# Thresholded attention and a gated MLP on one core: the MLP's products three steps earlier, in another order

## The chip, the cores and the metric

The kernel runs on one core of a Trainium2 chip. The metric is the time of one execution on the device, in microseconds (us). The profile is that of one such execution, and the trace is its list of instructions with their starts and durations. The engines are named as in the profile: PE is the matrix engine, PEld its weight loads, DVE the vector engine, ACT the scalar engine, POOL the general-purpose engine, and SP the queue that issues nearly all DMAs.

## The reference

Eight batches of eight heads, 576 rows of 64 numbers per head, all in float32. The first half is an attention whose weights are cut off below the row's maximum less `tau` (0.02):

```python
scores = scale * np.matmul(q, k.transpose(0, 1, 3, 2))
thresh = np.max(scores, axis=-1, keepdims=True) - tau
scores = np.where(scores >= thresh, scores, -1000000000.0)
scores = scores - np.max(scores, axis=-1, keepdims=True)
attn = np.exp(scores)
attn = attn / (np.sum(attn, axis=-1, keepdims=True) + 1e-09)
attn_out = np.matmul(attn, v)
```

The heads of a batch are put side by side (576 rows of 512 numbers, `x`), and the second half is a gated MLP on it:

```python
h = np.maximum(x @ w_in, 0.0)                      # 512 -> 1024
u, v = h[..., :512], h[..., 512:]
v_n = (v - mean(v)) / np.sqrt(var(v) + 1e-06)      # over the last axis
v_s = np.einsum('ts,bsd->btd', w_spatial, v_n) + b_spatial[None, :, None]
out = (u * v_s) @ w_out
```

## The kernel before

**Attention in 144 steps.** Two heads of one batch make a pair `i`, 32 pairs in all. A step `(i, c)` takes 128 of the 576 score rows of a pair. The last 64 rows of two neighbouring pairs share one step, `c = 4`, so an even pair has four steps and an odd pair has five, in the order 4, 0, 1, 2, 3. In `step()` the engines get this, in this order:

- PE: `scores()` (L545 and L550) into one of two score tiles `s` of three PSUM banks each; then the matmuls of the step's jobs.
- DVE: the row maxima `negm` (L586), for `c` = 2 and 4 a small correction (L590), and later the cut `p` (L567), which belongs to the step before and only exists for `c` = 0, 1, 3.
- ACT: the evacuations of the step's jobs, then `e` from the scores (L609; L603 with an `exp` of the whole row, L605, where `c` is 2 or 4). The pass over `s` is what frees the score tile for the step after next.
- SP: the transposes `pT<-p` by DMA, loads and outputs.

**Jobs.** Each step has a list `fs` of jobs, each with matmuls into one PSUM bank (`mm`) and an evacuation (`ev`) on ACT ("act") or DVE ("dve"). The list is sorted with the act jobs first. The matmuls of the first two jobs stand right behind the scores on PE, and their act evacuations stand on ACT ahead of the step's `e`. The matmuls of a third job stand behind the first two on PE. A third job's act evacuation is put into `held` and runs at the start of the next step. In the 144 steps a job's bank comes from `ps_f`, which has two banks in rotation: a job's matmuls wait until the job before the last has been evacuated.

Jobs that belong to the attention: `qk_main` and `qk_rem` transpose q and k of the next pair (L245, L260; evacuated by ACT at L250, L252, L263), `pv` and `pv_rest` multiply the weights by v (L289, L294; evacuated by DVE at L301, L303). `x_pe` (L367, ACT L374) transposes some pairs of `x`, and `ws_pe` (L388, ACT L392) the five pieces of `w_spatial`.

Jobs of the MLP of a batch:

- `v`, five per batch: `moe_v` (L418, ACT L428), with normalisation afterwards on ACT (L442, two steps later) and POOL; the fifth also carries the last output rows of the batch before (`ends`, L403 and L406, with a further copy at L432).
- `s`, five: `moe_s` (L490, or L495 for the fifth, which has 20 short matmuls), multiplied by `u` on DVE (L504, L507).
- `u`, five: `moe_u` (L460, or L465 for the fifth), ACT L475 or L477.
- `o`, four: `moe_o` (L519), ACT L524, then a DMA to the output.

**The order.** One batch is four pairs, so 18 steps. Job number `j` of `ORDER` of batch `b` goes to step `LAG + 18 * b + j`; `v` and `u` are those of batch `b`, `s` and `o` those of batch `b - 1`. What would fall behind step 143 goes into `last` and runs after the steps. Loads and casts of the weights are `chores` at fixed steps.

**The tail.** After step 143 the six banks of the score tiles join `ps_f` as eight banks for the jobs (`bank()`). `run()` takes the rest of the jobs of batch 6, the last `pv` and `x_pe` jobs, and `s` of batch 6; then `last_gmlp` does `v`, its normalisation, `s` and the output of batch 7, with `u` of batch 7 and the four `o` of batch 6 in between.

Of the kernel before, what the change touches and what calls it, by code (L numbers as in the profile page):

```python
# [17 lines left out]
def kernel(  # L18
# [21 lines left out]
    NPAIR = B * H // 2  # L40
# [187 lines left out]
    def bank16():  # L228

        return bank(BF16, 640)  # L230
# [77 lines left out]
    def pv(i, part):  # L308

        b, hp = divmod(i, HP)  # L310
        hold = {}

        def mm():
            t = hold["t"] = bank()
            for k in range(2):
                weigh(t, 130 * k, pts[i, part][:, k], v_ring[i % 4])

        def ev():
            if part == 0:
                xns[i] = xp.tile([P, 4, P], BF16, name="xn")  # L320
            xn = xns[i]
            divide(hold["t"], [(slice(0, P), 0, 4,
                                xn[:, 2 * part:2 * part + 2, :].rearrange(
                                    "p c (h d) -> p (c h) d", h=2))])
            if part == 1:
                if hp == 0:
                    xts[b] = xtp.tile([P, 4, 640], BF16, name="xT")
                if i in x_on_pe:
                    return
                sends.append(lambda: nc.sync.dma_start_transpose(  # L330
                    out=xts[b][:, hp, 0:512].rearrange("p (c s) -> p c s", s=P),
                    in_=xn.rearrange("p c d -> p (c d)")))
        return "dve", mm, ev
# [25 lines left out]
    def x_pe(i, rest=False):  # L359

        b, hp = divmod(i, HP)
        hold = {}

        def mm():
            t = hold["t"] = bank16()
            for c in range(4):
                nc.tensor.transpose(out=t[:, c * P:(c + 1) * P], in_=xns[i][:, c, :],  # L367
                                    identity=identb)
            if rest:
                nc.tensor.transpose(out=t[:, 512:640], in_=xns["rest", i // 2], identity=identb)  # L370

        def ev():
            if not rest:
                nc.scalar.copy(out=xts[b][:, hp, 0:512], in_=hold["t"][:, 0:512])  # L374
                return
            nc.scalar.copy(out=xts[b][:, hp, 0:256], in_=hold["t"][:, 0:256])
            nc.vector.tensor_copy(out=xts[b][:, hp, 256:512], in_=hold["t"][:, 256:512])
            nc.vector.tensor_copy(out=xts[b][:, hp - 1, 512:640], in_=hold["t"][:, 512:640])
        return "act", mm, ev
# [102 lines left out]
    def moe_s(b, f):  # L482
        hold = {}
        vn = vn_ring[b % 2]

        def mm():
            t = hold["t"] = bank()
            if f < 4:
                for c in range(5):
                    nc.tensor.matmul(out=t, lhsT=vn[:, c, f * P:(f + 1) * P],  # L490
                                     rhs=wsT[:, c, 0:512], start=(c == 0), stop=(c == 4))
            else:
                for g in range(4):
                    for c in range(5):
                        nc.tensor.matmul(out=t[:, g * 64:g * 64 + 64],  # L495
                                         lhsT=vn[:, c, g * P:(g + 1) * P],
                                         rhs=wsT[:, c, 512:576], start=(c == 0), stop=(c == 4))

        def ev():
            if f == 0:  # L500
                gs[b] = mw.tile([P, 4, S], BF16, name="gT")
            t = hold["t"]
            if f < 4:
                nc.vector.tensor_tensor(out=gs[b][:, f, 0:512], in0=t, in1=us[b][:, f, 0:512],  # L504
                                        op=ALU.mult)
            else:
                nc.vector.tensor_tensor(out=gs[b][:, :, 512:576],  # L507
                                        in0=t[:, 0:256].rearrange("p (f s) -> p f s", f=4),
                                        in1=us[b][:, :, 512:576], op=ALU.mult)
        return "dve", mm, ev  # L510
# [228 lines left out]
    chores[13] = (load_w_in, 3)  # L739
    for gs_, f in (((4, 5, 6, 17), shape_w_in),  # L740
                   ((20, 25, 30), load_ws), ((24, 26, 29, 31, 34), shape_ws),
                   ((36, 41, 46, 51), load_w_o), ((39, 44, 49, 54), shape_w_o)):
        chores.update({g: (f, j) for j, g in enumerate(gs_)})

    LAG = 26
    ORDER = "vsvsvsvssuvuouououo"
    jobs, last = {}, []
    for b in range(B):  # L750
        n = dict.fromkeys("vuso", 0)
        for j, t in enumerate(ORDER):
            f = {"v": moe_v, "u": moe_u, "s": moe_s, "o": moe_o}[t]
            if t in "uv" or b:
                g = LAG + PER * b + j
                job = (f, b - (t in "so"), n[t])
# [5 lines left out]
    Z = B - 1  # L762
# [1 line left out]
    for g, j in x_jobs:  # L764
        jobs.setdefault(g, []).append((x_pe, j))
    for j in range(5):
        jobs.setdefault((29, 33, 34, 42, 44)[j], []).append((ws_pe, j))
    with tc.manual_schedule():
        for w in (0, 1):
            for f in load(0, 1, w, (nc.sync, nc.scalar)[w]):  # L770
                f()
        make_identity(nc, identf)
        clear()
        nc.vector.memset(ntau, -float(tau))
        nc.vector.memset(mhalf, -0.5)
        nc.scalar.activation(out=ctau, in_=ntau, func=ACT.Exp)
        nc.vector.tensor_copy(out=identb, in_=identf)
        for w in (0, 1):
            for f in load(1, 1, w):
                f()  # L780
        for f in load(0, 2, 2):
            f()
        for j in range(3):
            load_w_in(j)
        for _ in range(14):
            nc.tensor.transpose(out=ps_f.tile([P, 512], F32, name="f")[:, 0:P], in_=identf,
                                identity=identf)
        shape_first()
        first()
        shape_qk(1)  # L790
        queue = []
        for g, (i, c) in enumerate(steps):
            if c == 2 and i + 2 < NPAIR:
                shape_qk(i + 2)
            if c == 0:
                shape_v(i)
            if c == 0 and i % 2 and i + 3 < NPAIR or g == 0:
                for w in range(3):
                    queue.extend(load(i + (3 if g else 2), 2, w))
            if g in chores:  # L800
                chores[g][0](chores[g][1])
            fs, small_ones = [], []
            if i + 1 < NPAIR and c < 3:
                fs.append(qk_rem(i + 1) if c == 1 else qk_main(i + 1, c // 2))
            if i and c == (2 if i % 2 else 3):
                fs.append(pv(i - 1, 0))
            if i > 1 and c == 4:
                fs.append(pv(i - 2, 1))
            if i % 2 and c == 3:
                fs.append(pv(i - 1, 1))  # L810
            if i % 2 and i > 1 and c == 1:
                small_ones = [pv_rest(i // 2 - 1)]
                fs += small_ones
            fs += [f(*a) for f, *a in jobs.get(g, [])]
            fs.sort(key=lambda f: (f[0] == "dve", f in small_ones))
            sends += queue[:1 if g > 3 else 2]
            del queue[:1 if g > 3 else 2]
            step(i, c, fs)

        def run(*fs):  # L820
            for f in fs:
                f[1]()
                f[2]()
                for f in sends:
                    f()
                sends.clear()
        while held:
            held.pop(0)()
        mask()
        inner.close()  # L830
        wide.append(ctx.enter_context(tc.tile_pool(name="ps_t", bufs=6, space=PSUM,
                                                  reuse_waits="tile")))
        for _, f in later:
            f()
        last = [f(b, j) for f, b, j in last]
        run(last[0], pv_rest(NPAIR // 2 - 1), *last[1:3], x_pe(NPAIR - 2), *last[3:6],
            pv(NPAIR - 1, 0), *last[6:], pv(NPAIR - 1, 1), moe_s(Z - 1, 0), moe_s(Z - 1, 1),
            x_pe(NPAIR - 1, True), *[moe_s(Z - 1, j) for j in range(2, 5)])
        rest = last_gmlp(Z)
        next(rest)  # L840
        run(moe_u(Z, 0), moe_u(Z, 1))
        next(rest)
        run(*[moe_u(Z, j) for j in range(2, 5)], *[moe_o(Z - 1, j) for j in range(4)])
        next(rest)
        next(rest, None)
# [35 lines left out]
```

## Time and profile before

| | us |
|---|---|
| median of three runs | 480.41 |
| the three runs | 479.06, 480.41, 481.51 |
| profiled execution, its own time | 480.41 |
| span of its instructions | 478.6 |

The profiled execution's own time is that of the median, and 1.8 us of it lie around the span. The granted clock of PE was 0.995 of full speed over the span. Steps can be found in the trace by the 144 instructions of L586: the first starts at 9.2 us, the last at 437.7 us. "Step of the cycle" below is the number of a step modulo 18.

### The profile page before, as it was taken

Reading aid. Unit: us, or ns where it says so; the run is one execution under the profiler, and the core shown is the slowest. Engines: PE = TensorE matmul, PEld = TensorE weight load, DVE = VectorE, ACT = ScalarE, POOL = GpSimd, SP = SyncE. Lnnn points to the kernel's source line nnn. Section 1 sums busy time; section 2 is a strip of 40 time slices with the busy share of each in tenths; the row PEclk is TensorE's granted clock in tenths of the full one; section 3 lists DMA queues with packets and bytes.
Section 4 is the critical chain, followed back from the end, with each engine's and each line's share of the span. In section 5 each row is a group of like instructions: output and inputs, shape, how many; then the busy total and the mean of one; then the engine's idle time right before and its main releaser. Section 6 shows DMA issues by size and latency. Waiting matters only on the chain.

```text
span 478.6 us, 9894 instructions
## 1 busy us (share of the span) xinstructions
PE 448.3 (94%) x3664; PEld 238.3 (50%) x3664; DVE 418.0 (87%) x563; ACT 382.2 (80%) x666; POOL 229.1 (48%) x403
## 2 busy tenths in 40 slices
PE   7788888889899999999999999999999999999995
PEld 4344444454554555554555545555554545545542
DVE  4999999989889997999889898899889998898573
ACT  4778777998879798788979898798978889797251
POOL 3462544784337553474427652475436743253021
PEclk9899999999999999999999999999999999999999
DMA  7999999979999799898988999997996999766523
GB/s 225 255 185 199 223 236 197 214 159 204 179 191 194 172 212 223 189 170 183 192 197 202 182 200 191 223 190 156 222 227 170 195 173 218 138 113 120 149 82 117
DMA packets 231120, 89.38 MB, mean 187 GB/s; under 512 B 200608, under 2 KB 225312, under 8 KB 231072
## 3 DMA queue, kind: packets, MB, share of 16 engines
q1 hardware_dynamic: 230416, 87.86, 87.2%
q8 instruction: 29, 0.48, 0.4%
q0 software_dynamic: 160, 0.52, 0.3%
q10 hardware_dynamic: 496, 0.36, 0.2%
q14 instruction: 19, 0.16, 0.1%
HBM read 33.31 MB, written 9.44 MB: 89 GB/s over the span
## 4 chain that ended last, share of the span: by engine, by line
PE 48%; DVE 23%; ACT 19%; issue 6%; DMA 2%; SPq 1%; POOL 0%; POOLq 0%; ACTq 0%; DVEq 0%
PE s L550 14%; DVE negm L586 10%; DVE p L567 8%; PE f L245 5%; ACT e L609 5%; PE s L545 4%; ACT e L603 4%; PE f L294 4%; PE f L519 4%; PE f L460 3%; ACT p L605 2%; ACT vrel L428 2%; PE f L490 2%; PE f L289 2%; ACT sq L442 1%
## 5 line engine op out<-in xcount | busy, mean ns | idle before, releaser
L586 DVE TENSOR_REDUCE negm<-s 128x2 f32<-128x1152 f32 x144 | 194.8, 1353 | 26.1 <-PE s L550 25.3
L550 PE MATMUL s<-qkT 64*128 64x512 f32 (+1 forms) x640 | 162.9, 639 | 0.0
L567 DVE SCALAR_TENSOR_TENSOR p<-e,ctau 128x1152 bf16<-128x1152 f32 x96 | 138.6, 1444 | 1.3 <-ACT e L609 1.2
L609 ACT ACTIVATE e<-s,negm 128x576 f32<-128x576 f32 x192 | 131.8, 741 | 7.1 <-DVE negm L586 6.8
L603 ACT ACTIVATE e<-s,negm 128x576 f32<-128x576 f32 x96 | 65.9, 738 | 20.9 <-DVE negm L590 11.6
L545 PE MATMUL s<-kd,qkT 128*128 128x128 f32 (+1 forms) x320 | 64.4, 304 | 15.6 <-ACT e L609 10.5
L268 POOL COPY kd<-qkT 64x64 f32<-64x64 f32 x62 | 31.7, 512 | 91.2 <-ACT qkT L263 89.4
L545 PEld LDWEIGHTS s<-kd,qkT 128*128 128x128 f32 (+1 forms) x320 | 44.4, 180 | 34.7 <-ACT e L609 20.2
L550 PEld LDWEIGHTS s<-qkT 64*128 64x128 f32 (+1 forms) x640 | 42.1, 174 | 18.3 <-issue 3.0
L436 POOL TENSOR_SCALAR nmean<-sm 128x1 f32<-128x1 f32 (+1 forms) x35 | 15.3, 437 | 69.7 <-ACT vrel L428 64.3
L294 PEld LDWEIGHTS <-pT 128*128 128x128 bf16 x1024 | 41.8, 97 | 7.3 <-issue 4.8
L294 PE MATMUL f<-v,pT 128*128 128x65 bf16 x992 | 44.9, 194 | 0.0
L136 POOL COPY qn<-ql 128x640 f32<-128x640 f32 x31 | 34.7, 1120 | 21.2 <-DMA ql<-in_k_dram 15.1
L605 ACT ACTIVATE p<-e 128x1152 bf16<-128x1152 f32 x32 | 37.3, 1165 | 1.0
L252 ACT COPY qkT<-f 128x512 f32<-128x512 f32 x31 | 18.2, 587 | 16.4 <-PE f L245 16.4
L490 PE MATMUL f<-wsT,vn 128*128 128x512 bf16 x125 | 31.1, 379 | 0.0
L448 POOL TENSOR_SCALAR vn<-vrel,rs,nm 128x512 bf16<-128x512 f32 (+1 forms) x34 | 28.7, 844 | 3.7
L289 PE MATMUL f<-v,pT 128*128 128x130 bf16 x124 | 27.2, 219 | 3.5 <-ACT qkT L252 1.6
L460 PE MATMUL f<-xT,w_in 128*128 128x512 bf16 x112 | 28.7, 380 | 0.9 <-DVE xn L303 0.8
L418 PE MATMUL f<-w_in,xT 128*128 128x512 bf16 x112 | 28.8, 380 | 0.0
L303 DVE TENSOR_TENSOR xn<-f,r 128x256 bf16<-128x256 f32 x62 | 26.3, 425 | 2.1
L428 ACT ACTIVATE vrel<-f 128x512 f32<-128x512 f32 (+1 forms) x34 | 20.1, 592 | 7.6 <-PE f L418 5.2
(165 smaller groups left out, 638.7 us busy)
## 6 DMA issues: line engine op xcount, KB each, us to landing
vl<-in_v_dram SPq DMA_DIRECT2D x16, 512.0 KB, 4.4
ql<-in_q_dram SPq DMA_DIRECT2D x15, 512.0 KB, 4.6
kl<-in_k_dram SPq DMA_DIRECT2D x15, 512.0 KB, 4.5
out_dram<-o SPq DMA_DIRECT2D x20, 256.0 KB, 3.4
uT<-in_moe_w_in_dram SPq DMA_DIRECT2D x3, 512.0 KB, 6.6
uT<-in_moe_w_spatial_dram SPq DMA_DIRECT2D x2, 576.0 KB, 5.0
vl<-in_v_dram SPq DMA_DIRECT2D x16, 64.0 KB, 4.1
pT<-p SPq DMA_TRANSPOSE x64, 5.5
```

The lines of the kernel that those rows point to most:

```text
L136: nc.gpsimd.tensor_copy(out=t, in_=ld_ring[i // 2 % 2][w][:, 2 * (i % 2):2 * (i % 2) + 2].rearrange("p h c d -> p c h d"))
L289: nc.tensor.matmul(out=t[:, at:at + 130], lhsT=pt[:, 4, :], rhs=vt[:, 4:6, :].rearrange("p b d -> p (b d)"), start=True, stop=False)
L294: nc.tensor.matmul(out=t[:, at + 65 * h:at + 65 * h + 65], lhsT=pt[:, 5 * h + j, :], rhs=vt[:, 6 * h + j, :], start=False, stop=(h == 1 an ...
L460: nc.tensor.matmul(out=t, lhsT=w_in[:, m, f * P:(f + 1) * P], rhs=xts[b][:, m, 0:512], start=(m == 0), stop=(m == 3))
L490: nc.tensor.matmul(out=t, lhsT=vn[:, c, f * P:(f + 1) * P], rhs=wsT[:, c, 0:512], start=(c == 0), stop=(c == 4))
L545: nc.tensor.matmul(out=view(s[rows], 512, [[448, 2], [1, 64]]), lhsT=qks[n][:, 0, m], rhs=kd_ring[n % 2], start=True, stop=True)
L550: nc.tensor.matmul(out=s[rows, 1024 * h:1024 * h + 512], lhsT=qks[n][hs, 0, m], rhs=qks[n][hs, 1, 0:512], start=True, stop=True)
L567: nc.vector.scalar_tensor_tensor(out=pt[:, c % 2, :], in0=ef, scalar=ctau, in1=ef, op0=ALU.is_ge, op1=ALU.mult)
L586: nc.vector.tensor_reduce(out=nm, in_=s, axis=AX.X, op=ALU.max, negate=True)
L603: nc.scalar.activation(out=e[:, h, :], in_=s[:, h, :], func=ACT.Prelu, bias=nm[:, h:h + 1], scale=by, alpha=1e30)
L605: nc.scalar.activation(out=pr_ring[i // 2 % 2] if c == 4 else p_ring[2 * (i % 2) + c // 2][:, c % 2], in_=e.rearrange("p h s -> p (h s)"), ...
L609: nc.scalar.activation(out=e[:, h, :], in_=s[:, h, :], func=ACT.Exp, bias=nm[:, h:h + 1])
```

## The change

`LAG` goes from 26 to 23 and `ORDER` gets another sequence. The first `v` of a batch stays where it was (step 8 of the cycle), since three `s` now stand before it. The transposes of `w_spatial`, and the loads and casts of `w_out`, move to earlier steps to suit. By step of the cycle, with the attention's jobs in the first row (`x_pe` and `ws_pe`, which only stand in the first two cycles, left out):

| step | 0 | 1 | 2 | 3 | 4 | 5 | 6 | 7 | 8 | 9 | 10 | 11 | 12 | 13 | 14 | 15 | 16 | 17 |
|---|---|---|---|---|---|---|---|---|---|---|---|---|---|---|---|---|---|---|
| attention | qk | rem | qk | pv | pv | qk | rem, pv_rest | qk, pv | pv | qk | rem | qk | pv | pv | qk | rem, pv_rest | qk, pv | pv |
| before | v4 | u1 | o0 | u2 | o1 | u3 | o2 | u4 | o3, v0 | s0 | v1 | s1 | v2 | s2 | v3 | s3 | s4 | u0 |
| after | u2 | o1 | u3 | o2 | u4 | o3, s0 | s1 | s2 | v0 | s3 | v1 | s4 | v2 | u0 | v3 | u1 | v4 | o0 |

(Numbers count from 0, so the fifth of a kind has the number 4.)

Three jobs of batch 6, the fifth `v`, the second `u` and the first `o`, thereby move from the tail into the 144 steps; and steps 41 to 43, which had `u`, a `ws_pe` and `u`, get three `s` of batch 0. In the tail's `run()` the remaining jobs, the last `pv`, `s` and `x_pe` come in another order: two `s` stand ahead of the last `pv`.

```diff
-                   ((36, 41, 46, 51), load_w_o), ((39, 44, 49, 54), shape_w_o)):
+                   ((35, 39, 43, 47), load_w_o), ((38, 42, 46, 50), shape_w_o)):
...
-    LAG = 26
-    ORDER = "vsvsvsvssuvuouououo"
+    LAG = 23
+    ORDER = "sssvsvsvuvuvouououo"
...
-        jobs.setdefault((29, 33, 34, 42, 44)[j], []).append((ws_pe, j))
+        jobs.setdefault((27, 29, 35, 37, 39)[j], []).append((ws_pe, j))
...
-            pv(NPAIR - 1, 0), *last[6:], pv(NPAIR - 1, 1), moe_s(Z - 1, 0), moe_s(Z - 1, 1),
-            x_pe(NPAIR - 1, True), *[moe_s(Z - 1, j) for j in range(2, 5)])
+            pv(NPAIR - 1, 0), moe_s(Z - 1, 0), moe_s(Z - 1, 1), pv(NPAIR - 1, 1),
+            moe_s(Z - 1, 2), x_pe(NPAIR - 1, True), moe_s(Z - 1, 3), moe_s(Z - 1, 4))
+        assert len(last) == 6, len(last)
```

## The prediction

> **What bounds the kernel now.** First the page: busy shares, and who is waited for.
>
> ```profile
> PE 448.3 (94%) x3664; PEld 238.3 (50%) x3664; DVE 418.0 (87%) x563; ACT 382.2 (80%) x666; POOL 229.1 (48%) x403
> ...
> L545 PE MATMUL s<-kd,qkT 128*128 128x128 f32 (+1 forms) x320 | 64.4, 304 | 15.6 <-ACT e L609 10.5 <-ACT e L603 2.8 <-ACT qkT L284 1.0
> ```
>
> PE leads, with DVE and ACT close. Shares hide stages, so next the windows by stage: before any MLP job, the first MLP cycle (steps 26 to 43), five full cycles, the last steps, the tail (columns: length, busy PE, PEld, DVE, ACT, POOL, clock, DMA share, GB/s).
>
> ```profile
> 79.85:132.40 52.55, 47.33 (x400) 25.82 (x400) 47.31 (x60) 47.99 (x87) 32.32 (x57) 1.00 0.96 188
> 132.40:187.75 55.35, 54.10 (x451) 28.79 (x450) 49.87 (x64) 47.45 (x85) 29.49 (x52) 1.00 0.94 198
> 187.75:409.19 221.44, 217.97 (x1793) 115.45 (x1792) 199.67 (x253) 189.78 (x337) 113.03 (x196) 1.00 0.93 194
> 409.19:437.70 28.51, 27.73 (x240) 14.56 (x238) 26.26 (x36) 23.01 (x42) 12.48 (x26) 1.00 0.66 124
> 437.70:478.60 40.90, 36.02 (x296) 18.37 (x292) 23.43 (x55) 16.40 (x31) 5.57 (x7) 0.98 0.42 116
> ```
>
> In a full cycle (55.2 us, as from 329.80 to 385.00, with PE busy for 54.5) PE hardly idles: PE sets the pace, and a wait put on PE costs its own length unless it replaces one. PE issues in order, so the question is which job waits for a bank. I therefore read the timeline of one cycle, engine by engine. Prices from start to start on PE: scores 1.46, qk 0.49, rem 0.16, pv 0.62, a full v, u or o 0.87, s 1.08, the fifth s 0.58, the fifth u 0.46, the fifth v (ends) 0.92.
>
> A rule speaks otherwise: the Trainium skill, Perfetto Trace Analysis, Identifying the Most-Contended Engine, says that matmul busy time is no good measure of PE and that weight-load busy time is; by that (PEld 50%) DVE would be the bound, its work is unchanged, and the time would stay at 480.4. I go by the gapless starts.
>
> **The jobs themselves.** Nothing is added or removed, only moved: instruction counts, DMAs and their sizes are the same. Three PE jobs leave the tail; by cycle step 5 three s have entered.
>
> **One full cycle, in five stretches** (R is the start of a step's L586).
>
> *From R of step 4 to the scores of step 8: 10.71 now (341.43 to 352.14).* After the change step 5 holds three jobs: qk, o, s. The s needs the bank of qk, and ACT evacuates qk only behind the two passes of step 4 (ACT, around that place):
>
> ```profile
> 341.27 1.37 ACT L609 ACTIVATE e<-s,negm 128x576 f32<-128x576 f32 x2
> 342.52 0.59 ACT L524 COPY o<-f 128x512 f32<-128x512 f32 x1
> 343.02 1.37 ACT L603 ACTIVATE e<-s,negm 128x576 f32<-128x576 f32 x2
> 344.43 1.16 ACT L605 ACTIVATE pr<-e 128x1152 bf16<-128x1152 f32 x1
> 345.50 0.58 ACT L250 ACTIVATE qkT<-f 128x512 f32<-128x512 f32 x1
> ```
>
> L250 ends at 346.08, 4.65 behind R. PE gets there sooner: fifth u 0.46, pv 0.62, scores 1.46, qk 0.49, o 0.87 make 3.90. So s waits 0.8 (0.4 if step 4 took as long as with today's o) and starts at 4.70; with s 1.08, scores 1.46 and 0.11 to DVE, R of step 6 is at 7.35. Step 6 (rem, s, pv_rest) is what step 15 is now, where DVE is the late one: its divide ends 4.08 behind R (374.89 to 378.97), and the pv of step 7 needs that bank. From 4.15: pv 0.62, s 1.08, so the scores of step 8 start at 7.35 + 5.85 = 13.2. **+2.5**, of it 1.5 more work (the fifth u, o and three s make 4.57, today's o, u, o and fifth u 3.07), the rest waits.
>
> *To R of step 9: 5.43 now (352.14 to 357.57).* Step 8 loses the o that stood beside v: **-0.85**.
>
> *To the scores of step 14: 13.0 now (357.57 to 370.57).* Step 11 gets the fifth s (0.58) for a full one (1.08), step 13 a u (0.87) for an s. PE gains nothing:
>
> ```profile
> 362.81 0.65 PE L245 MATMUL f<-identf,kn 128*128 128x128 f32 x4
> 363.30 1.24 PE L490 MATMUL f<-wsT,vn 128*128 128x512 bf16 x5
> 364.38 0.34 PE L545 MATMUL s<-kd,qkT 128*128 128x128 f32 x1
> ```
>
> The `e` of step 10 (ACT L609, 362.92, 1.36 long) frees the score tile at 364.28, so PE would arrive 0.5 earlier and wait 0.45; at step 13 likewise 0.2, behind the `e` of step 12. **0.**
>
> *To R of step 17: 12.1 now (370.57 to 382.68).* In step 15 pv_rest already waits for the copy of rem:
>
> ```profile
> 376.14 0.27 ACT L263 COPY qkT<-f 128x128 f32<-128x128 f32 x1
> ...
> 376.46 0.22 PE L289 MATMUL f<-v,ptr 128*128 128x130 bf16 x1 [0.28 <-ACT qkT L263]
> ...
> 378.38 0.59 DVE L303 TENSOR_TENSOR xr<-f,r 64x128 bf16<-64x128 f32 x2
> ...
> 379.12 0.22 PE L289 MATMUL f<-v,pT 128*128 128x130 bf16 x1
> ```
>
> L490 began at 374.94, so its 1.08 ended at 376.03 and the wait is 0.43. With u for s PE arrives 0.21 earlier, and the u of step 13, copied ahead of L603, puts ACT 0.29 later: the wait becomes 0.92. Against that, DVE, which holds R of step 17 today, sheds two products (L504 0.69, L507 0.42). Net **-0.3**.
>
> *To R of step 4: 13.95 now.* R of step 17 now lags the end of its scores by 0.78 (PE began u at 381.90), which shortens the next stretch by as much. Without the lag, o 0.87, pv 0.62 and scores 1.46 take 2.97 for 2.33. In step 16 ACT has qk, two evacuations of the fifth v, a square, L603 and L605: 0.49 + 0.59 + 0.6 + 0.7 + 1.4 + 1.07 = 4.85 against 3.5 of PE; by my count that adds only 0.15 in step 0 (bounds 0 and 1.2, the whole surplus; I stay near 0 because step 2 today has such a surplus, 4.1 against 2.9, and PE runs on without a gap). **+0.6.**
>
> Sum per cycle: 2.5 - 0.85 + 0 - 0.3 + 0.6 = +1.95, so about 57.1 for 55.2. Five cycles from step 44 to 134: **+9.7**. Bounds per cycle: +1.0 if the wait of step 5 is 0.4 and step 7's is hidden, +2.6 if ACT's surplus counts.
>
> The Trainium skill (Perfetto Trace Analysis, Matmuls) says that independent groups should rotate through different PSUM banks so that one's evacuation overlaps the next's matmuls. Three groups on two banks behind a long ACT pass break that; no row gives this wait for s itself.
>
> **Steps 26 to 43.** The same five v and five u, only sooner, and three s more (3.25 of PE). Up to step 38 the shuffled ws_pe and u come out within 0.3. In step 38 x_pe becomes the third job (qk, u, x_pe), so its copy is held until behind L605; today that pass runs 118.33 to 119.4, the copy takes 0.58, and the pv of step 39, which could start at 118.3, waits until 119.95: +1.6, and +0.6 for the u that moved ahead. Step 40 gets u, x_pe, pv for x_pe, pv: +0.4. Steps 41 to 43 with s each: step 42 about 4.1 for 3.43 (step 15's 4.11), step 43 some 0.3 longer: +1.0. Sum **+3.6**; bounds +1.7 (PE idles 3.5 there today, and half could be used) and +4.5.
>
> **Steps 134 to 143.** The o beside v is gone (-0.85), and steps 141 and 142, DVE-bound at 4.15 and 3.93, lose their products (-1.0): **-1.85.** The earlier loads of w_out queue on SP ahead of `pT<-p`; four of 256 KB, landing in 4.4 as now, hidden by four or more steps to their use; at worst 0.3 once.
>
> **Tail.** PE runs gapless from 437.77 to 464.7. Three jobs less are -2.6. The last pv needs `pT`, landing 8.85 behind the last R (446.55); in the new order PE arrives after 8.9, thanks to the two s ahead of it, so at most 0.2 is lost: **-2.4.**
>
> **Sum.** +3.6 + 9.7 - 1.85 - 2.4 = +9.0 on the profiled execution's 480.41, which is also the median: **489.4**. About 0.5% (2.4 us) is what a measurement can tell from no change.
>
> **Rivals.**
> *Faster: the idle of the first cycle swallows the jobs.* PE waits about 3.5 in steps 26 to 43. If the three s (3.25) fill that, the 2.6 that the steps gain is paid for, the full cycles stay at 55.2 and the tail's -2.4 remains: 480.4 + 2.6 - 3.2 - 2.4 = 477.4. For it: PE there is busy only 47.3 of 52.55. Against: DVE and ACT are as busy (47.3 and 48.0), and a third job's bank is freed by ACT. It decides if the s of step 5 and the pv of step 39 wait less than 0.1. Chance 0.07.
> *No change: waits only change places.* The 0.8 of step 5 is taken from what DVE would hold in steps 6 and 7 anyway; the cycles gain 0.3 each, the first cycle 1.7, and with -1.85 and -2.4 it is about 479.4. Chance 0.10.
> *Slower still: ACT in step 16.* If its surplus of 1.2 reaches PE each time, five cycles add 5 more: 494. For it: L609 and L603 are what L545 waits for on the page. Chance 0.13.
> My forecast: 0.70.
>
> **How the numbers follow.** Low end: +1.0 per cycle, +1.7 early, -1.85, -2.6: 482.7; down to 481 to take in part of the no-change case. High end: +2.6 per cycle, +4.5, -1.5, -2: 494.4, cut to 494. Range 481 to 494. Faster 0.07, same 0.10, slower 0.83.
>
> **What would show it.** In the profile after: cycles of about 57 between every eighteenth L586; L490 in step 5 behind ACT L250 by some 0.8; L289 in steps 7 (behind DVE L303) and 15 (behind L263, near 0.9); L545 in step 12 behind L609; L289 in step 39 behind L374; a tail from the last L586 of about 38.5 for 40.9. I am wrong if the cycles stay below 55.8, or if PE's waits in step 5 are under 0.3.

## The result and the profile after

The changed kernel took 494.23 us (median of four runs, 493.41 to 495.29); the kernel before, run beside it, took 479.74. The ratio is 1.030 with a 95% interval of 1.026 to 1.035: 14.5 us slower, where 9.0 were forecast, and just outside the range of 481 to 494. The profiled execution of the kernel after took 493.41 with a span of 491.6; all stretches below come from it, against the 480.41 and 478.6 of before. These two are 13.0 apart, the medians 14.5; the stretches can only account for the 13.0.

The page of the kernel after, as shown for before (busy us, share, count; then two groups: busy, mean ns, idle in front and what ended it):

```profile
PE 449.0 (91%) x3664; PEld 238.6 (49%) x3664; DVE 419.3 (85%) x563; ACT 382.6 (78%) x668; POOL 224.4 (46%) x407
...
L545 PE MATMUL s<-kd,qkT 128*128 128x128 f32 (+1 forms) x320 | 63.6, 302 | 15.7 <-ACT e L609 11.1
...
L490 PE MATMUL f<-wsT,vn 128*128 128x512 bf16 x130 | 32.1, 379 | 3.8 <-ACT qkT L250 3.8
```

PE, DVE and ACT are busy for as long as before (POOL for 4.7 us less); 13.0 us of waiting came on top. The wait in the last line is new: s now waits, always for the copy of qk, where in the page of before the same line ends in an idle of 0.0.

The windows by stage, cut at the same steps as before (length, busy PE, PEld, DVE, ACT, POOL, clock, DMA share, GB/s):

```profile
78.87:136.36 57.49, 51.10 (x422) 27.60 (x422) 50.21 (x62) 49.46 (x88) 32.10 (x57) 1.00 0.90 192
136.36:193.97 57.61, 54.62 (x450) 28.96 (x448) 50.39 (x65) 47.39 (x85) 28.00 (x51) 1.00 0.90 191
193.97:424.29 230.32, 218.48 (x1794) 115.84 (x1792) 201.55 (x253) 189.54 (x337) 107.69 (x196) 1.00 0.88 184
424.29:450.67 26.38, 25.87 (x222) 13.49 (x220) 24.44 (x33) 22.89 (x45) 11.35 (x24) 1.00 0.67 115
450.67:491.60 40.93, 33.93 (x294) 17.56 (x291) 23.41 (x55) 15.84 (x29) 8.56 (x14) 0.98 0.42 116
```

| stretch | before | after | difference | forecast |
|---|---|---|---|---|
| steps 17 to 25 | 25.16 | 24.17 | -0.99 | 0 |
| steps 26 to 43 | 52.55 | 57.49 | +4.94 | +3.6 |
| five cycles, steps 44 to 133 | 276.79 | 287.93 | +11.14 | +9.7 |
| steps 134 to 142 | 28.51 | 26.38 | -2.13 | -1.85 |
| tail, from the last L586 | 40.90 | 40.93 | +0.03 | -2.4 |

The -0.99 is not the change's: three later kernels made from before also took 24.2 there. A cycle is 57.59 for 55.36. In the tail PE does 2.1 us less (33.93 busy for 36.02) in the same time.

**Where PE waits in the cycle.** ACT around step 5, from the timeline:

```profile
354.11 1.16 ACT L605 ACTIVATE pr<-e 128x1152 bf16<-128x1152 f32 x1
355.18 0.58 ACT L250 ACTIVATE qkT<-f 128x512 f32<-128x512 f32 x1
```

and PE in steps 5, 7, 12 and 15, in order of time (start, length, what it does, the idle ahead of it and its releaser):

```profile
354.01 1.03 PE L519 MATMUL f<-w_o,gT 128*128 128x512 bf16 x4
355.81 1.24 PE L490 MATMUL f<-wsT,vn 128*128 128x512 bf16 x5 [0.76 <-ACT qkT L250]
...
362.88 0.22 PE L289 MATMUL f<-v,pT 128*128 128x130 bf16 x1 [0.65 <-DVE xr L303]
...
375.79 0.49 PE L545 MATMUL s<-kd,qkT 128*128 128x128 f32 x2 [0.29 <-ACT e L609]
...
388.15 0.22 PE L289 MATMUL f<-v,ptr 128*128 128x130 bf16 x1 [0.72 <-ACT qkT L263]
```

The lines with a wait are the four that were forecast, at their places and with their releasers (the third stands at the scores of step 12, which PE reaches early because of the short s in step 11). Against what usually passes from start to start they cost 0.93, 0.81, 0.45 and 0.88 (forecast: 0.8, for step 7 the place without a size, 0.45, 0.92). The first is a third group of matmuls in a step for which there are two banks: o ends at 354.88, but the bank of qk is only copied once ACT has done L603 and L605.

**Where PE waits in the tail** (PE, timeline):

```profile
452.91 0.22 PE L289 MATMUL f<-v,ptr 128*128 128x130 bf16 x1 [0.65 <-ACT o L524]
...
458.28 2.32 PE L490 MATMUL f<-wsT,vn 128*128 128x512 bf16 x10
462.15 0.23 PE L289 MATMUL t<-v,pT 128*128 128x130 bf16 x1 [1.55 <-DMA pT<-p]
```

After the two s PE stands still (1.71 from where s would have let it start) until the last `pT` lands. That transpose was issued 4.98 behind the last L586 (before: 4.27) and landed 11.44 behind it (before: 8.85): 0.71 later in issue and 1.88 longer under way.

### The profile page after: what moved, and what is told of

Read it like the earlier page. It is cut to its first block, busy times and chain, and to the rows that moved or that the text cites. A ratio compares the mean times of both kernels' runs of the same rounds, so it can differ in the third digit from the quotient of the medians.

```text
span 491.6 us, 9915 instructions
## 1 busy us (share of the span) xinstructions
PE 449.0 (91%) x3664; PEld 238.6 (49%) x3664; DVE 419.3 (85%) x563; ACT 382.6 (78%) x668; POOL 224.4 (46%) x407
## 4 chain that ended last, share of the span: by engine, by line
PE 38%; ACT 28%; DVE 19%; issue 10%; DMA 4%; POOL 0%; POOLq 0%; SPq 0%; ACTq 0%
PE s L550 12%; DVE negm L586 10%; ACT e L609 7%; ACT e L603 6%; DVE p L567 6%; PE f L490 4%; ACT sq L442 4%; PE s L545 4%; PE f L294 3%; PE f L245 3%; DMA pT<-p 3%; ACT p L605 3%; ACT vrel L428 2%; ACT qkT L250 2%; ACT pr L605 2%
## 5 line engine op out<-in xcount | busy, mean ns | idle before, releaser
L586 DVE TENSOR_REDUCE negm<-s 128x2 f32<-128x1152 f32 x144 | 194.9, 1354 | 33.7 <-PE s L550 33.3
L567 DVE SCALAR_TENSOR_TENSOR p<-e,ctau 128x1152 bf16<-128x1152 f32 x96 | 142.5, 1485 | 3.1 <-ACT e L609 2.9
L603 ACT ACTIVATE e<-s,negm 128x576 f32<-128x576 f32 x96 | 65.9, 741 | 25.9 <-DVE r L301 14.5
L268 POOL COPY kd<-qkT 64x64 f32<-64x64 f32 x62 | 16.8, 271 | 92.6 <-ACT qkT L263 90.9
L436 POOL TENSOR_SCALAR nmean<-sm 128x1 f32<-128x1 f32 (+1 forms) x35 | 17.7, 504 | 70.4 <-ACT vrel L428 67.1
L448 POOL TENSOR_SCALAR vn<-vrel,rs,nm 128x512 bf16<-128x512 f32 (+1 forms) x35 | 43.4, 1240 | 3.8
L136 POOL COPY qn<-ql 128x640 f32<-128x640 f32 x31 | 30.4, 980 | 17.4 <-DMA ql<-in_k_dram 9.2
L605 ACT ACTIVATE p<-e 128x1152 bf16<-128x1152 f32 x32 | 37.2, 1163 | 1.0
L490 PE MATMUL f<-wsT,vn 128*128 128x512 bf16 x130 | 32.1, 379 | 3.8 <-ACT qkT L250 3.8
L156 POOL CAST v<-vl 128x640 bf16<-128x640 f32 x32 | 35.3, 1103 | 0.4 <-DMA vl<-in_v_dram 0.4
L303 DVE TENSOR_TENSOR xn<-f,r 128x256 bf16<-128x256 f32 x62 | 26.3, 425 | 2.1
L460 PE MATMUL f<-xT,w_in 128*128 128x512 bf16 x104 | 26.8, 380 | 0.0
```

Source lines behind the costliest of these rows:

```text
L136: nc.gpsimd.tensor_copy(out=t, in_=ld_ring[i // 2 % 2][w][:, 2 * (i % 2):2 * (i % 2) + 2].rearrange("p h c d -> p c h d"))
L156: nc.gpsimd.tensor_copy(out=bass.AP(v_ring[i % 4].tensor, v_ring[i % 4].offset, [v_ring[i % 4].ap[0], [6 * (D + 1), 2], [D + 1, 5], [1, D] ...
L448: nc.gpsimd.tensor_scalar(out=dst, in0=vrel[:n], scalar1=rs[:n], scalar2=nm[:n], op0=ALU.mult, op1=ALU.add)
L490: nc.tensor.matmul(out=t, lhsT=vn[:, c, f * P:(f + 1) * P], rhs=wsT[:, c, 0:512], start=(c == 0), stop=(c == 4))
L567: nc.vector.scalar_tensor_tensor(out=pt[:, c % 2, :], in0=ef, scalar=ctau, in1=ef, op0=ALU.is_ge, op1=ALU.mult)
L586: nc.vector.tensor_reduce(out=nm, in_=s, axis=AX.X, op=ALU.max, negate=True)
```

## Experiments

Theories: (T1) PE waits for banks and score tiles that ACT, in order, frees late, and each such wait costs its length; (T2) DVE sets steps 6 to 8, so that a bank freed sooner there gains nothing; for the tail, queue order on SP, PE's order, ACT, or the DMA itself. Times are medians, ratios are to the kernel before with 95% intervals, cycles are means over steps 44 to 133 of the profiled execution.

### The third job of step 5 taken out

```diff
                 job = (f, b - (t in "so"), n[t])
+                if t == "o" and n[t] == 3:
+                    g += 3
```

> The kernel after, with the fourth o of a batch three steps later (step 8 of the cycle, beside v, where it stood before), so step 5 holds two jobs. Theory (the third group waits for a bank behind ACT's two passes): the wait of 0.93 at L490 goes, the pv of step 7 may still wait behind DVE, the work of o is the same: -0.5 to -0.9 per cycle, 3 to 5 us less than after. Rival (DVE would hold steps 6 and 7 anyway, as its rows stand without a gap there): step 6 begins sooner, step 8 not, cycle within 0.2 of 57.6 plus the o (0.87) now in step 8: 0 to +4 us.

488.95 us, ratio 1.018 [1.015, 1.021]; cycle 56.19 for 57.59. The group of s matmuls on its page has lost its wait:

```profile
L490 PE MATMUL f<-wsT,vn 128*128 128x512 bf16 x130 | 32.1, 379 | 0.0
```

Step 5 is 1.79 shorter (the wait and the 0.87 of o), step 6 is 0.29 shorter, and step 8 is 0.68 longer. So T1 holds for this wait, and more than the expected 0.9 is saved: o beside v in step 8 costs less than its PE time. This one placement is 1.4 of the 2.2 us that a cycle lost.

### Division ahead of the cut p on DVE

```diff
+        first = len(fs) > 2 and i % 2 and c == 1
+        if first:
+            for kind, mm, ev in fs[2:]:
...
         if unmasked:
             mask()
...
-        for kind, mm, ev in fs[2:]:
+        for kind, mm, ev in fs[2:] if not first else ():
```

> The kernel after, with pv_rest's matmuls and its division on DVE (L303) ahead of the cut p (L567) in the odd pairs' c = 1 steps (6 and 15 of the cycle). Theory A (the pv of the next step waits only for the bank that L303 frees): the 0.81 of step 7 goes, some 0.5 to 0.9 per cycle, 3 to 4 us less than after. Theory B (DVE has no gap from step 6 to step 8, so its order gives nothing): L289 in step 7 no longer waits, but the scores of step 8 start as late as now; within 1 us of after, or 1 to 2 us slower because p, and with it pT, comes 1.2 later.

493.86 us, ratio 1.029 [1.027, 1.032]; cycle 57.43. PE in steps 7 and 8 of this kernel (timeline):

```profile
362.65 0.22 PE L289 MATMUL f<-v,pT 128*128 128x130 bf16 x1
...
367.28 0.22 PE L289 MATMUL f<-v,pT 128*128 128x130 bf16 x1 [0.30 <-DVE gT L504]
```

The wait of step 7 is gone and another stands in step 8, again for DVE; the steps 6 to 8 take 10.51 for 10.67. The edit also acts in step 15, where the steps 15 to 17 take 10.79 with it and without it. In the kernel after DVE has indeed hardly a gap there (DVE, timeline):

```profile
358.37 1.36 DVE L586 TENSOR_REDUCE negm<-s 128x2 f32<-128x1152 f32 x1 [0.60 <-PE s L550]
359.70 0.69 DVE L504 TENSOR_TENSOR gT<-f,uT 128x512 bf16<-128x512 f32 x1
360.31 1.70 DVE L567 SCALAR_TENSOR_TENSOR p<-e,ctau 128x1152 bf16<-128x1152 f32 x1
...
362.14 0.59 DVE L303 TENSOR_TENSOR xr<-f,r 64x128 bf16<-64x128 f32 x2
362.76 1.36 DVE L586 TENSOR_REDUCE negm<-s 128x2 f32<-128x1152 f32 x1
...
366.71 1.35 DVE L586 TENSOR_REDUCE negm<-s 128x2 f32<-128x1152 f32 x1
```

From 358.37 to 366.71 each instruction starts as the one before it ends. T2 holds in these steps: the products of s, two steps running, fill DVE.

### Squares behind e, on after and on before

The block that runs the due normalisation (`due`, L595 to L598) was moved behind the `e` of the plain steps:

```diff
-        due = [f for n, f in later if n <= 0]
-        later[:] = [(n - 1, f) for n, f in later if n > 0]
-        for f in due:
-            f()
...
                 nc.scalar.activation(out=e[:, h, :], in_=s[:, h, :], func=ACT.Exp,
                                      bias=nm[:, h:h + 1])
+            due = [f for n, f in later if n <= 0]
+            later[:] = [(n - 1, f) for n, f in later if n > 0]
+            for f in due:
+                f()
```

Since the countdown now only runs in steps with a plain `e`, some squares also come a step later.

> The kernel after, with the two-step-old normalisation work (squares L442 and what follows) put on ACT behind the step's e instead of ahead of it. If PE waits because ACT, in order, frees score tiles and banks late (theory), the waits on PE at steps 11 to 15 of the cycle (0.45, 0.3 and 0.88) go: about -1.4 per cycle, so 55.9 to 56.4 for 57.6, some 6 to 8 us less than after. If DVE sets these steps (rival), they only change their names: cycle 57.3 or more, within 1.5 us of after.

490.56 us, ratio 1.022 [1.019, 1.025]; cycle 56.94. The waits ahead of the scores of steps 12 and 14 went, as T1 has it; that of step 15 grew from 0.88 to 1.25, because the squares now stand ahead of the next step's copies. Half of what was expected.

> The kernel before, with the same edit: squares behind the step's e. Theory: the wait of 0.43 in step 15 of the cycle goes and little else, since PE has no other gap there: cycle 54.8 for 55.3, -2 to -3 us against before. Rival (DVE holds the step that follows): no change, 480.

484.34 us, ratio 1.009 [1.006, 1.011]: a miss, of the other sign than expected. Step 16 takes 4.19 for 3.68 in each cycle, and in step 54 PE stands 1.97 for the cast of w_out (POOL L181), which now queues behind the delayed normalisation; step 54 takes 6.80 for 3.05, and part of that is a halved clock of PE behind this wait (last section). The wait of step 15, which was to go, grew in the trace from 0.28 to 0.62. What frees a tile sooner for one waiter makes another wait on the same in-order engine.

### The square of the third v one step later, on after and on before

```diff
-            later.append((2, rest))
+            later.append((3 if c == 2 else 2, rest))
```

> The kernel after, with the square of the third v of a batch (L442) one step later, in step 15 of the cycle behind the evacuations instead of in step 14 ahead of e. Theory (pv_rest in step 15 waits 0.88 for the copy L263, which ACT reaches late because of the u and the square in step 14): the wait falls to about 0.3, cycle 57.0 to 57.2 for 57.6, 2 to 3 us less than after. Rival (DVE holds steps 15 and 16): cycle 57.5 or more.

490.71 us, ratio 1.023 [1.019, 1.027]; cycle 56.89. The wait of step 15 falls to 0.18 and the cycle by 0.70.

> The kernel before, with the square of the third v of a batch one step later (step 15 of the cycle). If the wait of 0.43 in step 15 costs its length: cycle 55.0, 478 to 478.7. If DVE's division sets the steps that follow: no change, 479.5 to 480.5.

480.88 us, ratio 1.002 [1.000, 1.004]; cycle 55.55. The same edit on the same wait (0.43 there) gains nothing: step 15 stays at 4.10 and step 16 grows from 3.68 to 3.94. PE's wait for L263 is gone there too, but in steps 16 and 17 it now waits 0.33 and 0.27 for DVE (L303 and L507). In before, DVE works without a gap from 374.89 to 383.95, in steps 15 to 17, with two products of s (DVE, timeline):

```profile
376.22 0.69 DVE L504 TENSOR_TENSOR gT<-f,uT 128x512 bf16<-128x512 f32 x1
...
382.35 0.42 DVE L507 TENSOR_TENSOR gT<-f,uT 128x256 bf16<-128x256 f32 x1
```

After the change these are gone, DVE stands still in the same steps, and PE's wait counts:

```profile
386.35 1.36 DVE L586 TENSOR_REDUCE negm<-s 128x2 f32<-128x1152 f32 x1 [1.12 <-PE s L550]
387.97 1.45 DVE L567 SCALAR_TENSOR_TENSOR p<-e,ctau 128x1152 bf16<-128x1152 f32 x1 [0.27 <-ACT e L609]
```

So a wait has a price only where its engine is the last one.

### The x_pe of step 38 moved to step 36

```diff
-    x_jobs = ((10, 0), (14, 1), (19, 2), (23, 3), (31, 4), (38, 5), (40, 6))
+    x_jobs = ((10, 0), (14, 1), (19, 2), (23, 3), (31, 4), (36, 5), (40, 6))
```

> The kernel after, with the x_pe of step 38 in step 36 instead, where it is still a third job but behind an e without the long third pass (L605). Theory (the pv of step 39 waits for the copy L374, held until behind L605): the wait of 0.98 in step 39 goes, and with it 0.9 to 1.6 us of the time. Rival (DVE or ACT set the steps around it): within 0.4 us of after.

493.01 us, ratio 1.028 [1.024, 1.031]. From R of step 36 to R of step 44 it takes 26.48 for 27.34: -0.86 against the profile of after, and -1.2 in the medians. PE's idle of 1.67 in step 39 is gone, a smaller one of 1.29 stands in step 37. The wait in step 39 can have a second price, shown in the last section.

### Only the loads, casts and ws_pe moved, in before

```diff
-                   ((36, 41, 46, 51), load_w_o), ((39, 44, 49, 54), shape_w_o)):
+                   ((35, 39, 43, 47), load_w_o), ((38, 42, 46, 50), shape_w_o)):
...
-        jobs.setdefault((29, 33, 34, 42, 44)[j], []).append((ws_pe, j))
+        jobs.setdefault((27, 29, 35, 37, 39)[j], []).append((ws_pe, j))
```

> The kernel before with only the moves of the loads and casts of w_out and of the five w_spatial transposes (ws_pe). All theories: nothing, 479.5 to 481; if the moved loads delay a pT on SP, or a ws_pe costs more beside the jobs at its new step, up to +1.5 us.

481.69 us, ratio 1.004 [1.002, 1.006]: a miss, small but measured. In before's order the last ws_pe shares step 39 with u and pv, pv is the third group and waits 1.73 for the copy of u behind L605: step 39 takes 4.63 for 2.14. It is the mechanism of step 5 once more, at a place where these moves were not costed.

### The tail: outputs behind the last transpose

```diff
-        ready = sends[:]
-        sends.clear()
+        ready = [] if i == NPAIR - 1 and c > 1 else sends[:]
+        del sends[:len(ready)]
```

> The kernel after, with the two output DMAs of the last two steps (L433 and L528) issued behind the last transpose pT<-p (L571) on SP instead of ahead of it. Theory (the transpose lands 6.46 after its issue, for 4.58 in before, because the two outputs are in the DMA engines ahead of it): it lands 4.5 to 4.7 after its issue, PE's 1.71 of idle ahead of the last pv goes, tail 39.0 to 39.4 for 40.9, and 1.5 to 1.9 us less than after. Rival (the tail's end is set by another chain, or the transfer is slow for another reason): tail 40.6 or more, within 0.5 us of after.

494.06 us, ratio 1.029 [1.026, 1.033]; tail 40.70, and the transpose lands 6.24 after its issue although the two outputs now stand behind it on SP. The order on SP is not the cause.

### The tail: old order of the last pv

```diff
-            pv(NPAIR - 1, 0), moe_s(Z - 1, 0), moe_s(Z - 1, 1), pv(NPAIR - 1, 1),
-            moe_s(Z - 1, 2), x_pe(NPAIR - 1, True), moe_s(Z - 1, 3), moe_s(Z - 1, 4))
+            pv(NPAIR - 1, 0), pv(NPAIR - 1, 1), moe_s(Z - 1, 0), moe_s(Z - 1, 1),
+            x_pe(NPAIR - 1, True), *[moe_s(Z - 1, j) for j in range(2, 5)])
```

> The kernel after, with the old order at the end of the tail: the last pv ahead of the first two s instead of behind them. Theory (PE waits for the last pT, and the two s of 1.08 each fill that wait): PE waits some 3.9 for it, everything behind starts 2.0 to 2.2 later, tail about 43. Rival (PE's order does not set the tail's end): tail within 0.5 of 40.9.

496.02 us, ratio 1.033 [1.029, 1.038]; tail 42.93, as expected in size but not in its make-up: `pT` lands 4.61 after its issue here, PE idles 1.85, and then runs the two s at half clock (2.00 and 1.84 for 1.08 each). Of the 2.0 us by which this tail is longer, 1.7 are thus the half clock. Against the kernel of the next experiment, whose transpose is as quick and whose tail is 39.27, the old order costs 3.66, the idle and the half clock together. So PE's order does set the tail, and the same transfer, behind the same two outputs, is quick.

What differs between the quick and the late transposes is a packet that the DMA view counts under another queue. In the windows around the last transpose (for each queue packets, MB and share of the 16 DMA engines' time; then the transpose and its us from issue to landing), first after, with one instruction packet:

```profile
q1 hardware_dynamic: 2972, 1.73, 85.1%
q8 instruction: 1, 0.02, 0.7%
...
pT<-p SPq DMA_TRANSPOSE x1, 6.5
```

then before, with none:

```profile
q1 hardware_dynamic: 2966, 1.27, 86.5%
...
pT<-p SPq DMA_TRANSPOSE x1, 4.6
```

Packets on q8 are of 16384 bytes and come about every 250 matmul and weight-load instructions of PE. One starts 10.55 behind the last L586 in before and 11.44 in the kernel with the old order, after the transpose has landed; in after it starts 9.41 behind it, just ahead of the landing to be expected (4.98 + 4.6 = 9.55).

### The tail: 20 PE instructions fewer ahead of it

```diff
-        for _ in range(14):
+        for _ in range(4):
             nc.tensor.transpose(out=ps_f.tile([P, 512], F32, name="f")[:, 0:P], in_=identf,
```

> The kernel after with 4 instead of 14 warm-up transposes on PE at the very start: 20 PE instructions fewer, so that PE's later instruction fetches (packets of 16 KB on a DMA queue of their own) come some 10 matmuls later in the program. In after one such packet starts 9.41 behind the last R, while the last pT<-p is still in transfer, and that pT lands 6.46 after its issue; in before and in the kernel with the old tail order the packet starts 10.55 and 11.44 behind R, and pT takes 4.57 and 4.61. Theory (the packet holds up one of the engines that carry the transpose): it now starts after PE's wait, pT lands 4.6 after its issue, PE's idle of 1.71 ahead of the last pv shrinks below 0.2, tail 39.0 to 39.5 for 40.9. Rival (pT is late for another reason, the two outputs having been tried): pT lands 6.2 or more after its issue, tail 40.7 to 41.

494.51 us, ratio 1.030 [1.028, 1.033], but the tail is 39.27: the packet starts at 11.48, and the DMA view of the same stretch reads

```profile
q1 hardware_dynamic: 2693, 1.23, 98.4%
...
pT<-p SPq DMA_TRANSPOSE x1, 4.6
```

with PE going from s to the last pv without a wait:

```profile
461.64 2.32 PE L490 MATMUL f<-wsT,vn 128*128 128x512 bf16 x10
463.79 0.22 PE L289 MATMUL t<-v,pT 128*128 128x130 bf16 x1
```

So 1.67 of the tail's missing 2.4 is the meeting of an instruction packet with the last transpose. (The median does not fall: with fewer warm-up transposes the first L586 comes at 10.30 for 9.12.)

The same can be read all over the sixteen traces: 179 transposes `pT<-p` with such a packet starting 2.0 to 4.5 us behind their issue took 6.40 in the median, and the 576 with none from 1.5 us ahead of the issue to the landing took 4.96. Most of that cost nothing: in no kernel did PE wait for more than five of its 64 transposes.

### The tail: the last square out of ACT's way as well

```diff
+        for _ in range(4):
...
-            later.append((2, rest))
+            later.append((9 if b == B - 2 and c == 3 else 2, rest))
```

> The kernel with 4 warm-up transposes, and besides the last batch's square of the fourth v (L442, in step 142) behind the last step's work. Theory (the rest of what the tail failed to gain is ACT: v in step 142 and this square keep the copy of o, for which PE waits 0.65, and the last e, and with it p and pT): the wait on L524 falls by 0.5 to 0.6, the last p and pT come 0.5 to 0.6 sooner, tail 38.6 to 38.8 for 39.27. Rival (ACT is late there for other work): tail 39.1 to 39.4.

494.25 us, ratio 1.029 [1.026, 1.032]; tail 38.89. The wait for the copy of o is gone and p and the issue of pT come 0.71 sooner. But the transpose takes 5.11 for 4.60 here and lands only 0.21 sooner (why stays open), and s now waits 0.48 for the normalised v whose square was put off: -0.38 where 0.5 to 0.7 was expected. Packet and ACT together give back 2.04 of the 2.4.

### All of it together

Fourth o, square of the third v, x_pe and 4 warm-ups as above, and the squares of steps 0, 10 and 12 behind that step's `e`:

> The kernel after with what the runs so far point to: the fourth o three steps later, x_pe of step 38 in step 36, 4 warm-up transposes, the square of the third v one step later, and the squares of steps 0, 10 and 12 of the cycle behind that step's e instead of ahead of it. Theory (PE's waits behind ACT cost their length and add): cycle 56.2 - 0.35 - 0.5 = 55.2 to 55.5, first cycle some 1.5 less, tail 39.2, so 478 to 481. If waits only change places: cycle 55.9 or more, 483 or more.

481.04 us, ratio 1.003 [1.001, 1.005]: cycle 55.12, below before's 55.36; tail 38.82. 13.2 of the 14.5 us are back. What is left lies in steps 26 to 43 (56.00 for 52.55) and in the start with fewer warm-ups (first L586 at 10.50 for 9.20).

A second try had 14 warm-ups, and the q and k transposes of pairs 2 to 7 done twice in their place, x_pe in step 35, and the late square:

> The combination once more, with 14 warm-up transposes again; in their place the q and k transposes of pairs 2 to 7 are done twice (48 matmuls, 96 PE instructions more, in early steps where PE waits anyway), so that the instruction packets come some 5 us sooner in the program; x_pe(5) goes to step 35, and the square of a_late behind the last step. Theory: starts 1.2 earlier than c_all, step 37 without its idle of 1.29, tail 38.4 to 38.9: 478.0 to 479.3, 0.1 to 0.4% below before. If the doubled transposes cost PE's time after all, or a packet meets another transfer that PE waits for: 480 to 482.

481.61 us, ratio 1.003 [1.001, 1.006]: the doubled transposes cost 0.8 in the first steps, the x_pe in step 35 brought back a wait of 0.92, cycle 55.33, tail 38.99. No version beat the kernel before.

## Why the prediction was right or wrong

**Right.** Direction and mechanism: PE sets the pace, a group put third in a step waits for a bank behind ACT's long passes, and the four waits of a cycle stand where they were placed. By stretch, per cycle: R of step 4 to R of step 9 +1.77 (forecast +1.65), step 9 to R of step 17 -0.28 (-0.3), step 17 to R of step 4 +0.73 (+0.6). The two experiments on single waits confirm the reason (third job -1.40, step 15 -0.70 per cycle), and the one on DVE's order confirms that DVE holds steps 6 to 8. Steps 134 to 142 gained 2.13 for 1.85. By the rule of the Trainium skill that the prediction names (Perfetto Trace Analysis, Identifying the Most-Contended Engine), read by weight-load busy time, DVE would have been the bound and nothing would have changed; weight loads stay at 49% and the time rose by 3%, so here that measure alone misled. (The page names the matmul rate as a share of its peak beside it, which was not worked out here.)

**The step that failed: the tail, -2.4, which was 0.0.** The prediction took the landing of `pT` from before (8.85 behind the last R) as fixed and let PE arrive after it, so that at most 0.2 would be lost. Two things moved it. ACT gets the fifth v and its copy in step 142 ahead of the square and `e`, and o in 143 (ACT, timeline of after):

```profile
448.37 0.58 ACT L432 COPY o<-f 64x512 f32<-64x512 f32 x1
448.98 0.72 ACT L442 ACTIVATE sq<-vrel,nmean 128x512 bf16<-128x512 f32 x1
...
449.82 1.37 ACT L603 ACTIVATE e<-s,negm 128x576 f32<-128x576 f32 x2
```

So p comes and its transpose is issued 0.71 later (the prediction counted the jobs' PE time and not their ACT time there), and moving the square out of the way took the 0.71 back. And an instruction packet of PE, whose place shifts with the number of PE instructions ahead of it, met the transpose and cost 1.67. The second could not be read off the order of the jobs; that such a packet runs at 10.55 behind the last R, 1.7 after the landing, was in the trace of before.

**Mis-sized terms.** Steps 26 to 43: +4.94 for +3.6, outside its upper bound of 4.5. Steps 38 and 39 came as forecast (+2.24 for 2.2), and step 40 cost nothing for 0.4. Steps 41 to 43 cost 1.94 for 1.0, since steps 42 and 43 run at DVE's pace, 4.39 and 3.95 as in a full cycle. The steps up to 37 cost 0.75 for at most 0.3; the largest part is 0.68 in step 31, where pv is the third group behind u and x_pe and waits 0.84 for the copy of u. PE's idle there before was also not 3.5 but 5.2 (52.55 less 47.33), and the change did not use it up: after it, it is 6.4. Cycles: 2.23 for 1.95, five times 0.28. Together 1.4 + 1.3, and 2.4 from the tail; the -0.99 ahead of step 26 and -0.3 in the last steps go the other way. That is about the 4.0 between the 9.0 forecast and the 13.0 of the two profiled executions; what put the medians another 1.5 apart stays open.

Three figures of the working do not fit each other. ACT's surplus in step 16, 4.85 less 3.5, is 1.35 and not 1.2. The terms of the last stretch, 2.97 less 2.33 and 0.15, make 0.8 and not 0.6, and 0.73 was measured. And the upper bound of a cycle, +2.6, does not hold ACT's surplus, as it says: with 1.2 in place of 0.15 the sum is +3.0.

**The rivals.** The faster and the unchanged case fell with cycles of 57.6. "Slower still" had 494 for a wrong reason: the surplus of ACT in step 16 reaches PE as 0.2 in step 17 and 0.22 in step 0, not as 1.2.

## What to carry to other kernels

With two banks in rotation, a third group in a step costs its wait for the evacuation ahead of it, on an engine that works in order; look at what that engine is queued on (a step with a long pass is the worst place) before giving a step a third job. A wait on one engine has a price only where that engine is the last to finish in that step: the same edit on the wait at the same place gained 0.70 a cycle after and nothing before, where DVE was last. And a transfer that lands just in time in the old profile is not a constant: before counting on it, price what its producer's queue and everything else on the DMA engines will do.

## What the runs showed of the hardware that was not expected

**Instruction packets compete with transfers.** The Trainium skill, Runtime: NRT & Kernel Launch, Instruction fetch mechanics, calls the cost of crossing a 16 KiB block mostly hidden. Here it was hidden except where the packet met a transfer that PE was about to need: in seven kernels a packet started 9.1 to 9.4 behind the last L586, and the last transpose took 6.24 to 6.48; in eight others it started at 10.55 or later, and in one at 4.67, 0.4 behind the issue, and the transpose took 4.56 to 5.21. Why a packet that takes 0.92 delays the landing by 1.9 stays open.

**An idle of 1.7 us can halve PE's clock.** Step 39 of after waits 1.67. In ten kernels with an idle of 1.67 to 1.82 there, six went over to half clock for 3.41 us, 0.1 to 1.6 us behind the wait, and the others, after among them, did not. Windows of the 3.5 us behind that wait (same columns as above), first after, then the kernel with the outputs held back, which has the same code there:

```profile
119.60:123.10 3.50, 3.18 (x57) 2.02 (x57) 1.80 (x3) 2.54 (x6) 0.36 (x2) 1.00 1.05 188
```

```profile
119.50:123.00 3.50, 3.47 (x30) 1.65 (x29) 0.61 (x2) 1.85 (x3) 0.23 (x2) 0.51 1.18 202
```

At a clock of 0.51 PE gets through 30 matmuls for 57, and the steps 38 to 40 take 12.15 for 10.61 (11.68 to 12.15 in the six). Apart from the first 25 us and the end, no idle below 1.67 was followed by a drop in any profile; one of 1.97 (squares behind e, in before) and one of 1.85 (old order of the tail) were. The Trainium skill, TensorE: Matmul & The Clock Gate, Why this matters for your kernels, allows gaps of up to about 3 us; the measurement says that half of that can be enough. So the wait in step 39 can cost 1.1 to 1.5 on top of its length, and the profiled execution of after, at 493.41 below its median of 494.23, is one in which it did not.
